# Banded attention inside a feed-forward kernel: probabilities turned and split block by block, one padded product for the sinks, normalisation on GpSimd

## The chip, the cores and the metric

The kernel runs on one core of one Trainium2 chip. The metric is the device time of one execution in microseconds (us). Engines are named as in the profile: PE is TensorE, DVE VectorE, ACT ScalarE, POOL GpSimd, SP SyncE, which here only issues DMAs.

## What is computed

The inputs of the attention are q, k and v of shape (4, 8, 768, 64); every query sees the first `n_sink` keys (4 here; the kernel holds up to 16) and the last `window` keys up to itself (128). The 8 heads of a token, side by side, are a row of 512 numbers, and go through two feed-forward layers, with 2048 hidden numbers each.

```python
scores = scale * np.matmul(q, k.transpose(0, 1, 3, 2))
keep = is_sink | in_window            # pos < n_sink, or 0 <= rel < window
scores = np.where(keep, scores, -1000000000.0)
scores = scores - np.max(scores, axis=-1, keepdims=True)
a = np.exp(scores)
a = a / (np.sum(a, axis=-1, keepdims=True) + 1e-09)
attn_out = np.matmul(a, v)
x = attn_out.transpose(0, 2, 1, 3).reshape(B * S, H * D)
h = x @ w_in                          # first layer
x = (h - np.tanh(h)) @ w_out
h = np.maximum(x @ w_in2, 0.0)        # second layer
out = (h * h) @ w_out2
```

## The kernel before, in words

**Two parts of a number.** Most products are made with float32r operands: a float32 is split into a high part (a copy to float32r, on ACT) and a low part (the difference, on DVE or POOL), and a product is the sum of three: high by high, high by low, low by high. Heads 0 to 15 (`n < FULL`) use plain float32 in the attention; the 48 later heads use the parts.

**Tiles.** The 3072 tokens are cut into 8 tiles of T = 384 tokens, half a batch each. An even tile holds the first half of a sequence (`half` = 0), an odd tile the second. For each tile the first layer runs over 16 hidden chunks of 128: `mm1` gives a chunk (12 products of 384 columns into a bank of PSUM, two halves of 6), `act` takes tanh on ACT (`t`), `h - tanh` on DVE, and splits it (`gs`: ACT copy, DVE or POOL difference), `mm2` adds the chunk into four banks `acc` (12 products, two halves of 6), one chunk behind. Then all tiles go through the second layer in the same way, with no attention any more.

**The stream of heads.** PE executes its instructions in program order, and the order is written out: before each half of `mm1` and each half of `mm2` a hook calls `tick(pos)`, which puts the attention's steps of that place there. A chunk has four places, a head eight, so that the 8 heads of the next tile fill the 16 chunks of a tile. Heads of even tiles (half 0) pass in the odd tiles 1, 3, 5, heads of odd tiles (half 1) in tile 0 (plain float32) and in tiles 2, 4, 6. The stream runs OFF = 10 places ahead of the tile that needs it. On the other engines a scheduler sets the order.

**One head.** Its 384 queries are three units u of 128. A unit of kind 2 (all three of half 1, only the last of half 0) sees two blocks of 128 keys, the one before and its own, and 16 sink keys: 272 columns. Kind 0 sees one block, kind 1 two blocks of which the first is where the sinks lie. `split_qk` and `split_v` split q, k and v of the next head (ACT copies, POOL differences). `score` makes two products into `ps_s`, adds the mask on DVE; `exp` exponentiates on ACT with the row sums in `sm`. `recip` and `norm` normalise on DVE. For a unit of kind 2 `norm` **folds**: since a query sees of the block before only keys above its own place, and of its own block only keys up to it, both blocks' probabilities are added into 128 columns (L290, L291). `trans` transposes the folded block on PE into `ps_t`, splits it in two copies (ACT L349, DVE L350), and POOL unfolds it with the mask `above` (L353, L354). The sinks' probabilities of all units lie side by side in `s.sink` and are transposed at once, 32 rows for each unit. `av` makes for each unit one product of 256 columns (high and low P side by side) for each block of V (lhs: high V in the upper, low V in the lower half of its columns), and one product with 16 rows for the sinks (`pts`, `v_k`) ahead of them. `gather` adds the parts up into `xf` for units 0 and 1 together, and for unit 2 (ACT L408, DVE L409, L412); every second head `xf` is split into `x`, the next tile's input.

Of the kernel before, what the change touches and what calls it, by code (L numbers as in the profile page):

```python
# [47 lines left out]
def scalars(c):  # L48
    """n_sink and window as float32 on every partition."""
# [11 lines left out]
def band_fits(c):  # L61
    """1 if n_sink and window fit the banded path, else 0."""
# [10 lines left out]
def keep_masks(c, pool, shape_n, base, tag):  # L73
    """Where query base+p sees key j, 1.0, else 0.0."""
# [16 lines left out]
def band_masks(c):  # L91
    """What is added to the scores of the first, the second and any later query block."""
# [26 lines left out]
    c.above = cp.tile([P, 1, P], F32, tag="above", name="above")  # L119
    nc.vector.tensor_scalar(c.above[:, 0, :], d, 0.0, None, ALU.is_gt)  # L120
# [22 lines left out]
def split(c, dst, src, lo_eng):  # L143
    """float32 as the sum of two float32r parts."""
# [5 lines left out]
class Weights:  # L150
    """The chunks of one layer's two matrices, on chip as float32r parts."""
# [18 lines left out]
class Heads:  # L170
    """Banded attention of one head and one tile after another, cut into steps."""
# [14 lines left out]
    def load(self, n):  # L186
# [11 lines left out]
        if n % (2 * H) == 0 and n > 0:  # L198
            self.vs_raw = c.sb.tile([P, DM], I32, tag="w_bit", name="w_bit", bufs=3).bitcast(F32)[: 3 * SR].rearrange(
                "p (h d) -> p h d", d=D)  # L200
            nc.sync.dma_start(self.vs_raw, c.vs[b])

    def split_qk(self, n):
        c, nc, s = self.c, self.c.nc, self.st[n]
        j, b, half, h = self.coords(n)
        nk = (3 + half) * KB - NS
# [10 lines left out]
    def split_v(self, n):  # L217
        c, nc, s = self.c, self.c.nc, self.st[n]
        j, b, half, h = self.coords(n)
        if n < FULL:  # L220
            return
        nb = 3 + half
# [18 lines left out]
    def bank(self, n, i, tag, spare):  # L241
        """A bank; the banks of the products serve too while there are none."""
# [4 lines left out]
    def score(self, n, u):  # L247
        c, nc, s = self.c, self.c.nc, self.st[n]
        half = self.coords(n)[2]
        if u == 0:  # L250
            if n < H:
                t, pt = (slot(c, "wo", FC - 1 - (2 * n + i) % TMP, F32).rearrange("p a c -> p (a c)") for i in range(2))
                s.p = t[:, : 3 * WN].rearrange("p (u w) -> p u w", w=WN)
                s.pt0 = pt.rearrange("p (b q) -> p b q", q=P)
# [504 lines left out]
```

## Time and profile before

| | |
|---|---|
| median of 3 runs | 1366.1 us (1365.66 to 1366.31) |
| span of the profiled execution | 1364.8 us |
| PE busy | 1302.1 us, 95% of the span |
| DVE, ACT, POOL busy | 855.0, 629.3, 443.9 us (63%, 46%, 33%) |
| tile 0, us from the span's start | 44 to 167.9 |
| tile 1 (heads of half 0 in it) | 167.9 to 258.0 |
| tile 2 (heads of half 1 in it) | 258.0 to 360.3 |
| tiles 3, 5 and tiles 4, 6 | 90.1 us and 102.3 us each |
| last tile of layer one, and layer two | from 745.2 us |

The span is what the profiler saw from the first instruction to the last; the timed runs are 1.3 us longer. A tile's stretch is read by the first `mm1` product of each tile. In the view of windows, busy times of the engines are in the order PE, PE's weight loads, DVE, ACT, POOL, and the number behind them is the granted clock of TensorE as a share of full speed.

### The profile page before, as it was taken

What the parts mean: (1) busy time and instruction counts of PE and PEld (TensorE: products, weight loads), DVE (VectorE), ACT (ScalarE), POOL (GpSimd) and SP (SyncE); (2) the same over time, 40 slices, a digit from 0 to 9 for tenths busy, and PEclk for the clock granted to TensorE, in tenths of its full rate; (3) what the DMA queues carried; (4) which work ended last, traced back from release to release, by engine and by line L of the source; (5) the groups of instructions that cost most, each with busy time, mean ns of one, the idle gap of its engine ahead of it and who ended that gap; (6) DMA issues with size and microseconds to landing.
All of it is one profiled execution on the core that took longest, in us unless ns stands there. A gap on an engine that the chain in (4) does not pass through costs nothing.

```text
span 1364.8 us, 19807 instructions
## 1 busy us (share of the span) xinstructions
PE 1302.1 (95%) x7080; PEld 1185.5 (87%) x7080; DVE 855.0 (63%) x2012; ACT 629.3 (46%) x1604; POOL 443.9 (33%) x463
## 2 busy tenths in 40 slices
PE   7999999989999989999989989999999999999998
PEld 6788899878899888998889987799999999999997
DVE  8999688888788887878785799722222222222222
ACT  6666556545555545665544455423232223232222
POOL 1555534556434556435553254301010101010000
PEclk9999999999999999999999999999999999999999
DMA  9631211211211211212102851010100000000000
GB/s 365 247 115 58 91 52 56 79 38 46 70 49 56 79 34 46 70 53 75 60 1 84 273 182 61 12 35 12 36 18 29 23 25 24 24 13 24 10 15 26
DMA packets 31836, 90.87 MB, mean 67 GB/s; under 512 B 3792, under 2 KB 11984, under 8 KB 31728
## 3 DMA queue, kind: packets, MB, share of 16 engines
q1 hardware_dynamic: 31728, 89.51, 19.6%
q8 instruction: 58, 0.95, 0.3%
q14 instruction: 50, 0.41, 0.1%
HBM read 76.91 MB, written 12.58 MB: 66 GB/s over the span
## 4 chain that ended last, share of the span: by engine, by line
PE 59%; DVE 28%; ACT 6%; issue 5%; DMA 1%; SPq 0%; DVEq 0%; ACTq 0%
PE acc L504 18%; PE ps_h L470 13%; PE acc L502 6%; PE ps_v L470 5%; PE ps_t L470 5%; PE ps_s L470 5%; PE ps_v L382 4%; DVE p L291 4%; DVE p L290 4%; DVE w_bit L137 3%; DVE gs L147 3%; DVE sm L283 3%; DVE w_bit L136 2%; ACT p L278 2%; DVE w_bit L135 2%
## 5 line engine op out<-in xcount | busy, mean ns | idle before, releaser
L470 PE MATMUL ps_h<-x,wi 128*128 128x384 f32 x1776 | 363.1, 343 | 1.0 <-DVE t L482 1.0
L470 PEld LDWEIGHTS ps_h<-x,wi 128*128 128x128 f32 x1776 | 302.5, 188 | 6.5 <-DVE t L482 1.7
L502 PE MATMUL acc<-gs,wo 128*128 128x384 f32 x1440 | 288.4, 341 | 1.1 <-DVE gs L147 1.1
L502 PEld LDWEIGHTS acc<-gs,wo 128*128 128x128 f32 x1440 | 244.0, 188 | 2.5 <-DVE gs L147 1.4
L147 POOL TENSOR_TENSOR x<-xf,x 128x384 fp32r<-128x384 f32 x36 | 38.2, 1070 | 366.4 <-ACT x L146 366.2
L504 PE MATMUL acc<-wo,gs 128*128 128x512 f32 x576 | 146.3, 397 | 4.2 <-DVE gs L147 3.6
L147 DVE TENSOR_TENSOR gs<-t,gs 128x384 fp32r<-128x384 f32 x168 | 114.0, 679 | 56.8 <-ACT gs L146 56.8
L504 PE MATMUL acc<-wo,p 128*128 128x512 f32 x576 | 143.4, 393 | 1.2 <-DVE p L147 0.9
L278 ACT ACTIVATE p<-p,nm 128x272 f32<-128x272 f32 (+1 forms) x168 | 84.5, 503 | 104.2 <-DVE nm L271 97.2
L504 PEld LDWEIGHTS acc<-wo,gs 128*128 128x128 f32 x576 | 107.9, 190 | 26.0 <-DVE gs L147 4.6
L504 PEld LDWEIGHTS acc<-wo,p 128*128 128x128 f32 x576 | 107.1, 188 | 21.0 <-DVE p L147 1.4
L146 ACT ACTIVATE gs<-t 128x384 fp32r<-128x384 f32 x184 | 95.5, 519 | 43.6 <-DVE t L485 38.1
L353 POOL TENSOR_TENSOR pt<-pt,above 128x256 fp32r<-128x256 f32 x96 | 70.7, 737 | 133.9 <-DVE pt L350 133.9
L481 ACT ACTIVATE t<-ps_h 128x384 f32<-128x384 f32 x116 | 56.8, 490 | 73.0 <-PE ps_h L470 73.0
L470 PE MATMUL ps_t<-x,wi 128*128 128x384 f32 x432 | 81.7, 337 | 0.0
L470 PE MATMUL ps_v<-x,wi 128*128 128x384 f32 x432 | 81.6, 337 | 0.0
L470 PE MATMUL ps_s<-x,wi 128*128 128x384 f32 x432 | 81.5, 336 | 0.0
L470 PEld LDWEIGHTS ps_t<-x,wi 128*128 128x128 f32 x432 | 77.0, 189 | 2.7
L354 POOL TENSOR_TENSOR pt<-pt 128x256 fp32r<-128x256 f32 x96 | 76.8, 800 | 7.5
L470 PEld LDWEIGHTS ps_v<-x,wi 128*128 128x128 f32 x432 | 76.7, 188 | 2.8
L470 PEld LDWEIGHTS ps_s<-x,wi 128*128 128x128 f32 x432 | 76.6, 188 | 2.8
L271 DVE CUSTOM_DVE_ANT_0 p<-ps_s,m 128x128 f32<-128x128 f32 (+1 forms) x144 | 59.1, 410 | 27.7 <-PE ps_s L270 26.1
(140 smaller groups left out, 2083.8 us busy)
## 6 DMA issues: line engine op xcount, KB each, us to landing
qkv<-in_a_dram SPq DMA_DIRECT2D x32, 608.0 KB, 4.0
wi<-in_w_in_dram SPq DMA_DIRECT2D x32, 512.0 KB, 5.7
wo<-in_w_out_dram SPq DMA_DIRECT2D x32, 512.0 KB, 5.8
qkv<-in_a_dram SPq DMA_DIRECT2D x24, 504.0 KB, 3.6
x<-o SPq DMA_DIRECT2D x32, 192.0 KB, 1.9
xf<-x SPq DMA_DIRECT2D x32, 192.0 KB, 2.4
out_dram<-o SPq DMA_DIRECT2D x24, 256.0 KB, 2.1
wi<-in_a_dram SPq DMA_DIRECT2D x8, 504.0 KB, 8.2
```

The source lines that it names most:

```text
L146: nc.scalar.activation(dst[:, 0, :], src, AF.Copy)
L147: lo_eng.tensor_tensor(dst[:, 1, :], src, dst[:, 0, :].bitcast(F32), ALU.subtract)
L271: nc.vector.tensor_tensor_reduce(out=s.p[:, u, :w], in0=sc[:, :w], in1=self.masks[kind], op0=ALU.add, op1=ALU.min, scale=-SCALE, scalar=3. ...
L278: self.mark[n] = nc.scalar.activation(s.p[:, u, :w], s.p[:, u, :w], AF.Exp, bias=s.nm[:, u : u + 1], scale=-1.0, accum_out=s.sm[:, u : u + 1])
L290: nc.vector.tensor_scalar(s.p[:, u, KB:], s.p[:, u, KB:], s.sm[:, u : u + 1], None, ALU.mult)
L291: nc.vector.scalar_tensor_tensor(s.p[:, u, KB:], s.p[:, u, :P], s.sm[:, u : u + 1], s.p[:, u, KB:], ALU.mult, ALU.add)
L353: nc.gpsimd.tensor_tensor(a, b.bitcast(F32), c.above.to_broadcast([P, 2, P]), ALU.mult)
L354: nc.gpsimd.tensor_tensor(b, b.bitcast(F32), a.bitcast(F32), ALU.subtract)
L470: nc.tensor.matmul(h[:, :T], w[:, a, kc, :], x[kc][:, b, :], start=(kc == 0 and i == 0), stop=(kc == KC - 1 and i == 2))
L481: c.last_a = nc.scalar.activation(t, h[:, :T], AF.Tanh)
L502: nc.tensor.matmul(acc[m][:, :T], w[:, a, ts(m, P)], gs[:, b, :], **st)
L504: nc.tensor.matmul(acc[m], gs[:, b, ts(m, P)], w[:, a, :], **st)
```

## The change

P is no longer folded. A head of half 0 has five blocks of probabilities of 128 by 128, one of half 1 six (`parts`), ordered by block of keys. They are transposed three at a time at places 0 and 2 of the next head (`trans`), each group into one bank, and evicted by one ACT copy of 384 columns (high) and one DVE difference (low), into one buffer `pt` with high P and low P apart. At place 4 the sinks' columns of each unit are transposed 64 rows high (`trans_sinks`); the high part goes to rows 0 to 63 of `pts`, the low part to rows 64 to 127, where the sink rows of V stand a second time, the rest being zeros (`layout`). `av` at places 3 and 5 makes for each block of V two products, one with high P and one with low P, over the queries of both units that see it (256 columns, or 128 columns at the ends, where the low one has only 66 of V's columns as outputs), all into one bank for the head. `av_sinks` at place 6 is a single product with 128 rows. `gather` is one ACT copy and one DVE addition of 384 columns. `norm` adds 1e-9 on ACT, takes the reciprocal on DVE, and multiplies on POOL, three instructions a head, all issued at place 5. The low part of `x` moves from DVE to POOL. OFF becomes 11; `pt` and `pts` have one buffer in place of two, and `o`, the buffer of the products' last eviction, two in place of three. The first weight conversions wait for head 3 in place of head 2.

```diff
-SR = 32               # rows, of which the sinks take the first, of a query block's sink probabilities when transposed
+SR = 64
...
-TRANS = ((1, 3, 5), (0, 3, 6))
-AV = ((4, 6, 9), (3, 7, 9))
-OFF = 10              # places by which the stream of heads runs ahead of the tile that needs it
+OFF = 11
...
-    def recip(self, n):
-        nc.vector.tensor_scalar(s.sm, s.sm, 1.0e-9, None, ALU.add)
+    def norm(self, n):
+        c, nc, s = self.c, self.c.nc, self.st[n]
+        nc.scalar.activation(s.sm, s.sm, AF.Identity, bias=c.eps)
         self.markd[n] = nc.vector.reciprocal(s.sm, s.sm)
...
+        for u in range(3):
+            w = self.width(n, u)
+            nc.gpsimd.tensor_scalar(s.p[:, u, :w], s.p[:, u, :w], s.sm[:, u : u + 1], None, ALU.mult)
+
+    def parts(self, n):
+
+        half = self.coords(n)[2]
+        out = []
+        for kb in range(3 + half):
+            for u in (kb - half, kb - half + 1):
+                if 0 <= u < 3:
+                    out.append((u, 0 if self.kind(n, u) == 0 or u + half != kb else KB, kb))
+        return out
+
+    def evict(self, n, hi, lo, src):
+
+        nc = self.c.nc
+        nc.scalar.activation(hi, src, AF.Copy)
+        if n >= FULL:
+            nc.vector.tensor_tensor(lo, src, hi.bitcast(F32), ALU.subtract)
+
+    def trans(self, n, g):
+
+        c, nc, s = self.c, self.c.nc, self.st[n]
+        bl = self.parts(n)
+        if g == 0 and n >= H:
+            pt = c.sb.tile([P, 2, 6, P], F32R, tag="pt", name="pt", bufs=1)
+            s.pt = pt if n >= FULL else pt.bitcast(F32)
+        lo, hi = 3 * g, min(3 * g + 3, len(bl))
+        tp = self.bank(n, g, "ps_t", "acc").rearrange("p (a q) -> p a q", q=P)
+        for i in range(lo, hi):
+            u, col, _ = bl[i]
+            nc.tensor.transpose(tp[:, i - lo, :], s.p[:, u, col : col + P], c.ident)
+        self.evict(n, s.pt[:, 0, lo:hi, :], s.pt[:, 1, lo:hi, :] if n >= FULL else None, tp[:, : hi - lo, :])
...
+        for i, u in enumerate(us):
+            nc.tensor.transpose(tp[:rows, i, :], s.p[:, u, P : P + rows], c.ident)
...
+            s.ps = c.sb.tile([P, 3, P], F32R, tag="pts", name="pts", bufs=1)[:, : len(us), :]
...
+        self.evict(n, s.ps[:rows], s.ps[SR:], tp[:rows, : len(us), :])
...
+            st = dict(start=(kb == 0), stop=False, skip_group_check=True)
...
+            v = s.vt[:, kb].rearrange("p a d -> p (a d)")
+            nc.tensor.matmul(s.av[:, cols], v, s.pt[:, 0, blocks, :], **st)
+            st["start"] = False
+            m = P if len(idx) > 1 else D + 2
+            nc.tensor.matmul(s.av[:m, cols], v[:, :m], s.pt[:, 1, blocks, :], **st)
...
+        nc.tensor.matmul(out, lhs, s.ps, start=False, stop=True, skip_group_check=True)
...
+        t = c.sb.tile([D, T], F32, tag="t_av", name="t_av", bufs=2)
+        nc.scalar.activation(t, s.av[D:, :T], AF.Copy)
+        nc.vector.tensor_tensor(dst, s.av[:D, :T], t, ALU.add)
...
+            split(c, x, self.xf, c.nc.gpsimd)
...
+            if k == 5:
+                self.norm(n)
+        m = n - 1
+        if 0 <= m < last:
+            if k in (0, 2):
+                self.trans(m, k // 2)
+            if k == 4:
+                self.trans_sinks(m)
+            if k in (3, 5):
+                self.av(m, k // 5)
...
+                self.av_sinks(m)
+                self.gather(m)
+                self.finish(m)
...
-                o = c.fp.tile([P, 512], F32, tag="o", name="o", bufs=3)
+                o = c.fp.tile([P, 512], F32, tag="o", name="o", bufs=2)
...
-                with tc.issue_after(heads.mark[2].ins), tc.issue_after(heads.markd[2].ins):
+                with tc.issue_after(heads.mark[3].ins), tc.issue_after(heads.markd[3].ins):
...
+    vs = np.zeros((B, P, H, D), v.dtype)
+    vs[:, :NS] = vs[:, SR : SR + NS] = v[:, :, :NS].transpose(0, 2, 1, 3)
+    arrays["vs"] = vs
```

The order of instructions on PE, before, for most of a head of half 1 in tile 2 (L470 is `mm1`, L502 `mm2`, L269 and L270 the scores, L327 and L330 transposes, L382 the products with V; the sizes are inputs' rows by columns):

```order
L470 MATMUL ps_h<-x,wi_776 128x384 x6
L382 MATMUL ps_v<-pts,v_k 128x256
L382 MATMUL ps_v<-pt,v_s 128x256 x2
L470 MATMUL ps_h<-x,wi_776 128x384 x6
L269 MATMUL ps_s<-k_h,q_s 128x272
L270 MATMUL ps_s<-k_l,q_s 128x272
L327 MATMUL ps_t<-ident,p 128x128
L330 MATMUL ps_t<-ident,p 96x128
L502 MATMUL acc<-gs,wo_734 128x384 x6
L382 MATMUL ps_v<-pts,v_k 128x256
L382 MATMUL ps_v<-pt,v_s 128x256 x2
L502 MATMUL acc<-gs,wo_734 128x384 x6
```

And of the change, from the second group of transposes of such a head to its product with the sinks (L437 is `mm1`, L469 `mm2`, L260 and L261 the scores, L308 and L321 transposes, L349, L352 and L363 the products with high P, low P and the sinks):

```order
L308 MATMUL ps_t<-ident,p 128x128 x3
L469 MATMUL acc<-gs,wo_1324 128x384 x6
L349 MATMUL ps_v<-pt,v_s 128x128
L352 MATMUL ps_v<-pt,v_s 66x128
L349 MATMUL ps_v<-pt,v_s 128x256
L352 MATMUL ps_v<-pt,v_s 128x256
L437 MATMUL ps_h<-x,wi_1440 128x384 x6
L260 MATMUL ps_s<-k_h,q_s 128x272
L261 MATMUL ps_s<-k_l,q_s 128x272
L321 MATMUL ps_t<-ident,p 64x128 x3
```

The three blocks of one product with the sinks and two with V, each into a bank that waits for the gathering of the last, became two groups of four products with V and one product with the sinks; transposes went from four to nine.

On ACT before, around the splitting of q, k for the next head in tile 2 (L481 is tanh, L212 and L214 the high parts of q and k, L278 exp, L146 the high part of `gs`, L349 of P, L408 the copy in `gather`):

```order
L481 ACTIVATE t<-ps_h 128x384
L212 ACTIVATE q_s<-qkv 128x384
L278 ACTIVATE p,sm<-p,nm 128x272
L146 ACTIVATE gs<-t 128x384
L214 ACTIVATE k_h<-qkv 128x560
L349 ACTIVATE pt<-ps_t 128x128
L408 ACTIVATE t_av<-ps_v 64x256
```

And of the change, at the same stretch of a head (L269 is exp, L206 the high part of q, L448 tanh, L274 the addition of 1e-9 to the sums, L217 the high part of v, L141 that of `gs`, L376 the copy in `gather`, L293 a group's high part of P):

```order
L269 ACTIVATE p,sm<-p,nm 128x272
L206 ACTIVATE q_s<-qkv 128x384
L448 ACTIVATE t<-ps_h 128x384
L274 ACTIVATE sm<-sm,eps 128x3
L217 ACTIVATE v_s<-qkv 128x4x64
L141 ACTIVATE gs<-t 128x384
L376 ACTIVATE t_av<-ps_v 64x384
L293 ACTIVATE pt<-ps_t 128x384
```

The addition to the sums, on which the reciprocal and the multiplications wait, stands behind a tanh, and the copy of v ahead of `gs`.

On POOL before, for most of a head in tile 2 (L353 and L354 unfold P, L213, L215 and L225 are the low parts of q, k and v):

```order
L354 TENSOR_TENSOR pt<-pt 128x256
L213 TENSOR_TENSOR q_s<-qkv,q_s 64x384
L215 TENSOR_TENSOR k_l<-qkv,k_h 128x560
L353 TENSOR_TENSOR pt<-pt,above 128x256
L354 TENSOR_TENSOR pt<-pt 128x256
L353 TENSOR_TENSOR pt<-pt,above 128x256
L354 TENSOR_TENSOR pt<-pt 128x256
L225 TENSOR_TENSOR v_s<-qkv,v_s 128x4x64
```

And of the change (L209, L207 and L218 are the low parts of k, q and v, L278 `norm`, L142 the low part of `x`):

```order
L209 TENSOR_TENSOR k_l<-qkv,k_h 128x560
L207 TENSOR_TENSOR q_s<-qkv,q_s 64x384
L218 TENSOR_TENSOR v_s<-qkv,v_s 128x4x64
L278 TENSOR_SCALAR p<-p,sm 128x272 x3
L142 TENSOR_TENSOR x<-xf,x 128x384
L209 TENSOR_TENSOR k_l<-qkv,k_h 128x560
```

The six unfolding instructions of a head are gone, and three multiplications stand behind the low part of v.

## Rows read from the trace of the kernel before

**Rows 1.** The page: span, and DMAs of the results with us to landing.

```profile
span 1364.8 us, 19807 instructions
...
out_dram<-o SPq DMA_DIRECT2D x24, 256.0 KB, 2.1
```

**Rows 2.** Windows (columns as told above): start, tile 0, tile 1, tile 2.

```profile
0.00:44.00 44.00, 35.99 (x204) 27.42 (x205) 36.27 (x146) 29.97 (x95) 9.87 (x15) 1.00 0.88 341
44.00:167.90 123.90, 115.61 (x663) 103.60 (x663) 106.58 (x211) 75.86 (x179) 68.43 (x53) 1.00 0.32 115
167.90:258.00 90.10, 87.08 (x522) 82.78 (x521) 73.64 (x208) 53.49 (x159) 38.32 (x44) 1.00 0.19 61
258.00:360.30 102.30, 94.77 (x537) 84.97 (x537) 83.65 (x221) 54.56 (x161) 59.61 (x70) 1.00 0.16 51
```

**Rows 3.** Waits of PE in tile 2: us in total, times, longest.

```profile
PE ps_v L382 <- DVE xf L412: 7.5, 8, 1.2
```

**Rows 4.** Waits of PE in tile 1.

```profile
PE ps_v L382 <- DVE xf L412: 3.0, 8, 1.4
```

**Rows 5.** Timeline of PE in tile 1: start, us, work.

```profile
232.46 0.28 PE L269 MATMUL ps_s<-k_h,q_s 128*128 128x272 f32 x1
...
232.71 2.25 PE L502 MATMUL acc<-gs,wo 128*128 128x384 f32 x12
234.79 0.27 PE L327 MATMUL ps_t<-ident,p 128*128 128x128 f32 x1
```

**Rows 6.** Timeline of PE and ACT at the end of tile 1.

```profile
254.23 0.51 PE L470 MATMUL ps_h<-x,wi 128*128 128x384 f32 x2
...
254.73 0.35 PE L382 MATMUL ps_v<-pts,v_k 16*128 16x256 f32 x1
...
255.35 0.27 PE L327 MATMUL ps_t<-ident,p 128*128 128x128 f32 x1
...
255.38 1.31 PE L470 MATMUL ps_h<-x,wi 128*128 128x384 f32 x6
...
256.73 0.49 ACT L481 ACTIVATE t<-ps_h 128x384 f32<-128x384 f32 x1 [0.71 <-PE ps_h L470]
...
257.12 0.52 ACT L212 ACTIVATE q_s<-qkv 128x384 fp32r<-128x384 f32 x1
```

**Rows 7.** The chain that ended last, in tile 0: start, us, what.

```profile
49.39 0.33 PE ps_t L327 x3
...
89.30 2.02 DVE w_bit L136 x2
...
96.17 0.60 DVE w_bit L136
...
133.99 2.03 DVE w_bit L136 x2
```

**Rows 8.** Groups of instructions on POOL: busy us, mean ns of one, idle before.

```profile
L147 POOL TENSOR_TENSOR x<-xf,x 128x384 fp32r<-128x384 f32 x36 | 38.2, 1070 | 366.4 <-ACT x L146 366.2
...
L354 POOL TENSOR_TENSOR pt<-pt 128x256 fp32r<-128x256 f32 x96 | 76.8, 800 | 7.5
...
L225 POOL TENSOR_TENSOR v_s<-qkv,v_s 128x256 fp32r<-128x256 f32 x24 | 17.4, 724 | 6.2 <-ACT v_s L224 6.2
L225 POOL TENSOR_TENSOR v_s<-qkv,v_s 128x192 fp32r<-128x192 f32 x24 | 14.8, 617 | 35.2 <-ACT v_s L224 35.2
...
masks.py:199 POOL TENSOR_SCALAR_AFFINE_SELECT ident<-ident 128x128 f32<-128x128 f32 x1 | 0.3, 292 | 0.0
```

**Rows 9.** Timeline of POOL in tile 0.

```profile
104.08 1.42 POOL L147 TENSOR_TENSOR gs<-t,gs 128x384 fp32r<-128x384 f32 x1 [1.98 <-issue]
```

**Rows 10.** Timeline at the end of the kernel: evictions of the last products.

```profile
1356.84 0.60 ACT L513 ACTIVATE o<-acc 128x512 f32<-128x512 f32 x1 [3.08 <-PE acc L504]
...
1358.20 0.60 ACT L513 ACTIVATE o<-acc 128x512 f32<-128x512 f32 x1 [0.76 <-PE acc L504]
```

More of the change, by code (lines that the diff above doesn't have):

```diff
@@ L204, in split_qk @@
         c, nc, s = self.c, self.c.nc, self.st[n]
-        j, b, half, h = self.coords(n)
-        nk = (3 + half) * KB - NS
+        nk = (3 + self.coords(n)[2]) * KB - NS
         if n < FULL:
@@ L296, in norm_sinks @@
-    def norm_sinks(self, n):
-        c, nc, s = self.c, self.c.nc, self.st[n]
-        if n < FULL:
-            return
-        us = [u for u in range(3) if self.folded(n, u)]
-        off = 0 if us[0] == 0 else P
-        s.nk = SR * len(us)
-        s.sink = s.p[:, 0, off : off + s.nk]
-        nc.vector.tensor_tensor(s.sink.rearrange("p (u k) -> p u k", k=SR), s.p[:, us[0] :, P : P + SR],
-                                s.sm[:, us[0] :, None].to_broadcast([P, len(us), SR]), ALU.mult)
-    def folded(self, n, u):
-        return n >= FULL and self.kind(n, u) == 2
@@ L385, in gather @@
-    def gather(self, n, u):
-        c, nc, s = self.c, self.c.nc, self.st[n]
-        j, b, half, h = self.coords(n)
-        if h % 2 == 0 and u == 1:
-            self.xf = c.sb.tile([P, T], F32, tag="xf", name="xf", bufs=2)
-        if n < FULL:
-            if u == 2:
-                nc.scalar.activation(self.xf[D * (h % 2) : D * (h % 2) + D, :], s.av[:D, :T], AF.Copy)
-        else:
-            self.add_up(n, u)
-        if u == 2:
-            if h % 2 == 1:
-                x = c.xp.tile([P, 2, T], F32R, tag="x", name="x", bufs=8)
-                split(c, x, self.xf, nc.vector if n >= H else nc.gpsimd)
-                self.x.setdefault(j, [None] * KC)[h // 2] = x
-            del self.st[n]
@@ new lines, in with_sinks, with trans_sinks @@
+    def with_sinks(self, n):
+        return [u for u in range(3) if self.kind(n, u) == 2]
+    def trans_sinks(self, n):
+        c, nc, s = self.c, self.c.nc, self.st[n]
+        us = self.with_sinks(n)
+        full = n < FULL
+        rows = P if full else SR
+        tp = self.bank(n, 0, "ps_t", "acc").rearrange("p (a q) -> p a q", q=P)
+        for i, u in enumerate(us):
+            nc.tensor.transpose(tp[:rows, i, :], s.p[:, u, P : P + rows], c.ident)
+        if n < H:
+            s.ps = s.pt[:, 0, 5:6, :]
+        else:
+            s.ps = c.sb.tile([P, 3, P], F32R, tag="pts", name="pts", bufs=1)[:, : len(us), :]
+            if full:
+                s.ps = s.ps.bitcast(F32)
+        self.evict(n, s.ps[:rows], s.ps[SR:], tp[:rows, : len(us), :])
@@ new lines, in av @@
+    def av(self, n, g):
+        c, nc, s = self.c, self.c.nc, self.st[n]
+        bl = self.parts(n)
+        if g == 0:
+            s.av = self.bank(n, n, "ps_v", "acc")
+        for kb in range(bl[-1][2] + 1):
+            idx = [i for i, x in enumerate(bl) if x[2] == kb]
+            if (idx[-1] >= 3) != g:
+                continue
+            u0 = bl[idx[0]][0]
+            cols = slice(u0 * P, (u0 + len(idx)) * P)
+            blocks = slice(idx[0], idx[-1] + 1)
+            st = dict(start=(kb == 0), stop=False, skip_group_check=True)
+            if n < FULL:
+                nc.tensor.matmul(s.av[:, cols], s.v[:, kb : kb + 2, :].rearrange("p a d -> p (a d)"),
+                                 s.pt[:, 0, blocks, :], **st)
+                continue
+            v = s.vt[:, kb].rearrange("p a d -> p (a d)")
[3 more added lines that the diff above has]
+            nc.tensor.matmul(s.av[:m, cols], v[:, :m], s.pt[:, 1, blocks, :], **st)
@@ L412, in add_up, with gather @@
-        nc.vector.tensor_tensor(dst, s.av[:D, :m, 0, :], t[:, :m, :], ALU.add)
+        us = self.with_sinks(n)
+        out = s.av[:, us[0] * P : 3 * P]
+        if n < FULL:
+            lhs = self.vsink[:, h : h + 2, :].rearrange("p a d -> p (a d)")
+        else:
+            lhs = self.vsink[:, h].rearrange("p a d -> p (a d)")
+        nc.tensor.matmul(out, lhs, s.ps, start=False, stop=True, skip_group_check=True)
+    def gather(self, n):
+        c, nc, s = self.c, self.c.nc, self.st[n]
+        h = self.coords(n)[3]
+        if h % 2 == 0:
+            self.xf = c.sb.tile([P, T], F32, tag="xf", name="xf", bufs=2)
+        dst = self.xf[D * (h % 2) : D * (h % 2) + D, :]
+        if n < FULL:
+            nc.scalar.activation(dst, s.av[:D, :T], AF.Copy)
+            return
+        t = c.sb.tile([D, T], F32, tag="t_av", name="t_av", bufs=2)
+        nc.scalar.activation(t, s.av[D:, :T], AF.Copy)
+        nc.vector.tensor_tensor(dst, s.av[:D, :T], t, ALU.add)
@@ L414, in tick, with finish @@
+    def finish(self, n):
+        c = self.c
+        j, b, half, h = self.coords(n)
+        if h % 2 == 1:
+            x = c.xp.tile([P, 2, T], F32R, tag="x", name="x", bufs=8)
+            split(c, x, self.xf, c.nc.gpsimd)
+            self.x.setdefault(j, [None] * KC)[h // 2] = x
+        del self.st[n]
     def tick(self, pos):
```

151 lines of the change are left out of this document (23 added, 128 removed).

## The prediction

> **What bounds the kernel now.** I read the windows of the first stages first [rows 2]. PE is busy for 94.77 of the 102.30 us of tile 2 and for 87.08 of the 90.10 us of tile 1, at a granted clock of 1.00, which is the 2.4 GHz level, throughout. So after tile 0 a tile lasts as long as PE's own work and its few waits, and DVE (83.65 and 73.64 us) is the nearest other engine. Tile 0 lasts 123.90 us, with DVE at 106.58: another bound, to which I come below. From 745 us on there is no attention, and the change touches nothing there but the buffers of the last eviction.
>
> Second, PE's waits. In tile 2 they come to 7.5 us in 8 waits, all at the first product of a block into `ps_v` that the addition into `xf` has not yet released [rows 3]; in tile 1 to 3.0 us [rows 4]. That is .94 us a head of half 1 and .38 a head of half 0.
>
> Third, what one PE instruction costs, from start to start in the timeline. Twelve products of 384 columns take from 232.71 to 234.79, .174 each [rows 5], so a tile's 384 products of `mm1` and `mm2` alone are 66.9 us. Two score products of 256 to 272 columns take from 232.46 to 232.71, .12 each [rows 5]. Three transposes take .33, .11 each [rows 7]. The block of one product with the sinks (16 rows) and two with V is dearer than three times .12: two `mm1` products start at 254.23, so that they end their issue at 254.58, and the next transpose starts at 255.35; the block took .77 without any wait in it [rows 6], .41 more than .36.
>
> **The change, per head of half 1** (24 heads, tiles 2, 4, 6; 12.79 us a head now, from 102.30/8). Off: three such blocks, -2.32; the waits on `xf`, -.94, since one bank now gathers a whole head and the next head's first product comes five places later. On: four products of 256 columns, +.48; the product with the sinks, 384 columns, +.17; four products of 128 columns, which I take at .12 (the transposes, 128 columns too, took .11; half the price of 256 columns, .06, is the other bound), +.48; five more transposes, +.55. This is -1.58, if nothing new waits. I assume here that the .41 belongs to the product with 16 rows, of which none is left.
>
> A new wait is likely, since the normalisation leaves DVE for the end of a queue. Call E the end of the first half chunk's products at place 5; it is 256.69 in [rows 6]. There tanh began .04 behind E and the next ACT instruction at E+.43. In the changed order that next one is the addition of 1e-9 (.1), then the copy of v (about .40 for 256 columns, by .52 for 384): done at about E+.96. POOL then splits v, .72 [rows 8], to E+1.73, and only then normalises, three units one after another.
>
> What one multiplication by a column on POOL costs, no row shows. POOL's differences of two inputs took .617 for 192 and .724 for 256 columns [rows 8]: .0017 a column and a fixed .30, which gives .75 for 272, or .78 with the .80 of L354. The only operation with one input, 128 wide, took .29 [rows 8], which is the fixed part alone. So .30 to .78; I take .50, between the two. The unit 0 is then ready at E+2.28. Its successor is pushed: DVE's difference for `gs` falls there, and when both engines read two inputs from SBUF they slow each other: a POOL difference of 384 columns took 1.42 beside a DVE weight conversion against a mean of 1.07 [rows 8, 9], and the conversion's pairs took 1.01 each against .60 alone [rows 7]. With that .35, unit 1 is ready at E+3.16, PE hears of it at 3.25.
>
> PE on its side issues after E the sinks' product, .17, twelve products, 2.09, the next scores, .24, and two transposes, .22; since its last product ends its issue .16 before E, it comes to the third transpose, the first of unit 1, at E+2.56. It waits .69 a head. Behind it in PE's queue stands all of the next chunk, so nothing fills this; DVE's eviction of the low part comes later by the same.
>
> Sum: -1.58 +.69 = -.89; with rounding -.90 a head, **-21.6 us** in 24 heads.
>
> **Per head of half 0** (24 heads; 11.26 us a head now, from 90.10/8). Off: one block with sinks, -.78, three other products, -.36, the wait, -.38. On: four products of 256 columns, +.48; two of 128 and the sinks' 128, +.36; one transpose, +.11. The wait at the norm: the first unit is 128 wide (.30), v's difference .617 [rows 8], and unit 1 is wanted at the second transpose, so it is due at E+2.40 and comes at about E+2.84: +.44. Sum -.14, **-3.4 us**.
>
> **Tile 0** (heads 8 to 15 in plain float32). The chain returns to the weight conversions of DVE, whose pairs come at 89.30 and 133.99 three heads apart, 14.90 us a head, and they are long just where POOL works [rows 7, 9]. The change takes the multiplications and part of the evictions off DVE and puts three POOL instructions and nothing else in their place, so DVE's own time falls and that in which POOL slows it rises, by .5 each. I take 14.2 to 15.0 a head in place of 14.9, **-2** (-5 to +6). Start: the heads of tile 0 have no products beside them, PE is busy 35.99 of 44.00 and DVE 36.27, and the DMA queues .88 [rows 2], so less DVE work meets the loads: **0**, -5 to +5, as the first product of layer one now stands one place later in the stream.
>
> **The end.** With two buffers `o` the third eviction of the last tile, at 1358.20, waits for the first, which starts at 1356.84 and takes .60 [rows 10], and for its DMA, 2.1 to land [rows 1]: 1359.5, **+1.4**. In the other tiles of layer two the next tile's work goes on meanwhile. Edits at nothing: `gather`'s one copy of 384 columns, the low part of `x` on POOL (1.07 every second head), behind the norms; POOL loses six instructions a head, three of them of .80 [rows 8], so it has the room (59.61 of 102.30 busy [rows 2]). That cover is gone if the norms cost far more (below).
>
> **The sum** is -21.6 -3.4 -2 +1.4 = -25.6: a span of 1339.2 in place of 1364.8 [rows 1], and 1.3 more by the timed runs: 1340.5, say **1341 us**. The 128-column products at .06 would take 10 more off (24 by .24 and by .18).
>
> On the unknown price: the Trainium skill, "GPSIMD Engine Reference", section "4.1 Engine selection", puts elementwise work on VectorE and calls GpSimd about twice slower for two inputs and about line-rate for one. By the first the change is a bad trade, by the second the multiplication would be near the lower bound above. No row here shows an instruction of this kind, so the sum keeps its bounds.
>
> **The rivals.** *All hidden.* ACT may bring the copy of v earlier, or a multiplication may take .30: then both new waits go, -.69 and -.44 a head, 27 us more: 1314. For it: POOL is then less busy than now; against: `gs` and v stand ahead. Chance .14.
>
> *Norms late (slower).* If a multiplication costs as much as a difference of two inputs, .78, unit 1 comes .56 later and tile 0's POOL work grows as well. Each .1 costs two times .1 for 24 heads of half 1, .15 for 24 of half 0 (its first unit is narrow), and .26 a head in tile 0: 4.8+3.6+2.1 = 10.5 us. From .50 to .78 that is 29 us: about 1370. It decides from .74 on. For it: all POOL work of 256 columns that is seen takes .72 or more. Chance .18.
>
> *The short product is not the cause.* If the .41 of a block comes not from 16 rows but from any change of shape between products, it comes back with the products of 66 columns (two a head of half 1, one of half 0): +.82 and +.41, 29.5 us: about 1370. Against it: transposes and scores between products of other widths go at .11 and .12. For it: only this block is seen with it. Chance .12. The Trainium skill, "TensorE: Matmul & The Clock Gate", section "Why this matters for your kernels", says that a product with 32 rows takes the time of one with 128, which would leave the 16 rows without blame; the block's .77 against .36 rather speaks against it.
>
> **How the numbers follow.** The forecast itself .50, all hidden .14, norms late .18, the shape .12, other causes (a race for `ps_t`, one buffer of `pt`, tile 0 by more than bound) .06. A difference under 0.2% (2.7 us) could not be told from none. Faster: .50 + .14, and .05 of the two rivals near 1370 and of the rest; same: .08; slower: .23, the most of the two rivals. The range goes from the all-hidden case, 1314, to 1374, a few us past the two slow ones; the forecast's own range is 1325 to 1356.
>
> **What would show it.** Right: tile 2 at about 95 us and tile 1 at about 89; no wait on `xf` at `ps_v`; waits of PE at the second or third transpose on POOL's multiplication, .4 to .7 a head; multiplications at .4 to .6; the sinks' product at .17 to the next. Wrong: multiplications over .74; products of 66 columns with gaps; tile 0 over 130 us; waits on DVE's low parts of P at `av`, because `pt` has one buffer and DVE writes it after ACT.

## The result: slower by 0.65%

The changed kernel takes 1375.86 us (median of 4 runs, 1372.14 to 1376.34) against 1366.2 before: a ratio of 1.0065, 95% interval 1.0051 to 1.0079. The forecast was 1341 with a range up to 1374. The profiled execution of the changed kernel took 1376.34, with a span of 1374.5, 9.7 more than before [rows 1].

The busy times on its page answer to the table of before: PE and DVE have less to do, POOL 63.8 us more, and the span is longer all the same.

```profile
PE 1294.6 (94%) x7152; PEld 1196.3 (87%) x7152; DVE 633.9 (46%) x1376; ACT 643.9 (47%) x1588; POOL 507.7 (37%) x491
```

Where the time went is read best by stages that begin exactly with the first `mm1` product of a tile. Behind the start, the windows of [rows 2] and the table of before do not: they were cut some 4 us later (167.90 for 163.84 and so on; 745.2 for 738.70 at the last), so that tile 0 has 123.90 us there and 119.72 here, and the other tiles differ by a few tenths. The kernel before, cut exactly (its start is 44.12 us): tile 0, tile 1, tile 2, tile 7.

```profile
44.12:163.84 119.72, 111.43 (x638) 99.42 (x637) 103.96 (x203) 73.34 (x172) 67.64 (x52) 1.00 0.32 115
163.84:253.53 89.69, 86.67 (x522) 82.78 (x521) 72.90 (x205) 52.99 (x158) 36.01 (x42) 1.00 0.18 60
253.53:356.14 102.61, 95.08 (x538) 85.19 (x537) 83.95 (x222) 54.35 (x159) 60.71 (x72) 1.00 0.17 53
...
738.70:805.47 66.77, 65.36 (x374) 64.43 (x373) 49.28 (x73) 32.99 (x65) 21.30 (x17) 1.00 0.78 248
```

The changed kernel, its start and the same four tiles:

```profile
0.00:61.76 61.76, 41.59 (x180) 29.03 (x181) 24.51 (x104) 35.88 (x113) 33.19 (x42) 0.93 0.66 251
61.76:188.15 126.39, 107.55 (x571) 93.63 (x570) 88.78 (x158) 78.91 (x189) 95.86 (x80) 0.98 0.31 110
188.15:277.81 89.66, 86.98 (x541) 84.39 (x540) 43.33 (x122) 52.49 (x150) 49.26 (x53) 1.00 0.20 62
277.81:373.20 95.39, 91.82 (x575) 88.38 (x574) 48.22 (x122) 57.11 (x151) 54.24 (x53) 1.00 0.18 56
...
741.35:814.26 72.91, 67.86 (x373) 66.90 (x373) 49.38 (x72) 32.15 (x64) 20.25 (x16) 0.95 0.72 224
```

Start +17.6, tile 0 +6.7, tile 1 nothing, tile 2 -7.2, tile 7 +6.1. With tiles 4 and 6, which lose 7.2 each too, and .9 us behind tile 7, this is the whole difference. The gain in the heads of half 1 is there. Three other stages take it back: the start and tile 0, which serve the first 16 heads, and tile 7, which has no attention beside it.

PE's waits in the changed kernel, the start (two rows), tile 0 (two), tile 2, tile 7 (us in total, times, longest).

```profile
PE ps_t L308 <- POOL wo L278: 6.9, 12, 1.3
...
PE acc L308 <- POOL wo L278: 4.4, 8, 0.9
...
PE ps_v L363 <- ACT pts L293: 6.5, 5, 2.1
...
PE ps_t L308 <- POOL p L278: 4.6, 3, 3.6
...
PE ps_t L308 <- POOL p L278: 3.2, 7, 0.5
...
PE acc L469 <- ACT o L480: 3.7, 1, 3.7
```

In the start and in tiles 0 and 2 the name is the same: the multiplication of L278 on POOL. Its price, in groups by shape (busy us, mean ns, idle before), for heads 8 to 63 (`p`) and for the first eight (`wo`):

```profile
L278 POOL TENSOR_SCALAR p<-p,sm 128x272 f32<-128x272 f32 x144 | 146.9, 1032 | 8.2 <-DVE sm L275 8.2
...
L278 POOL TENSOR_SCALAR wo<-wo,sm 128x272 f32<-128x272 f32 x16 | 16.0, 1012 | 0.0
...
L278 POOL TENSOR_SCALAR wo<-wo,sm 128x128 f32<-128x128 f32 x8 | 5.5, 691 | 19.0 <-DVE sm L275 15.1 <-PE acc L363 2.1 <-PE ps_v L363 1.8
```

1.03 us for 272 columns: twice my .50, and beyond the .78 that I took for the upper bound.

### The profile page after: what moved, and what is told of

Its sections match the earlier page's. It is cut to its first block, busy times and chain, and to the rows that moved or that the text cites. A ratio compares the mean times of both kernels' runs of the same rounds, so it can differ in the third digit from the quotient of the medians.

```text
span 1374.5 us, 19167 instructions
## 1 busy us (share of the span) xinstructions
PE 1294.6 (94%) x7152; PEld 1196.3 (87%) x7152; DVE 633.9 (46%) x1376; ACT 643.9 (47%) x1588; POOL 507.7 (37%) x491
## 5 line engine op out<-in xcount | busy, mean ns | idle before, releaser
L437 PE MATMUL ps_h<-x,wi 128*128 128x384 f32 x1776 | 365.6, 344 | 0.0
L437 PEld LDWEIGHTS ps_h<-x,wi 128*128 128x128 f32 x1776 | 307.4, 190 | 4.5 <-DVE t L449 1.3
L469 PE MATMUL acc<-gs,wo 128*128 128x384 f32 x1440 | 301.4, 346 | 9.4 <-ACT o L480 6.0
L469 PEld LDWEIGHTS acc<-gs,wo 128*128 128x128 f32 x1440 | 247.6, 189 | 15.9 <-ACT o L480 7.7
L142 POOL TENSOR_TENSOR x<-xf,x 128x384 fp32r<-128x384 f32 x64 | 66.9, 1051 | 345.1 <-ACT x L141 342.9
L278 POOL TENSOR_SCALAR p<-p,sm 128x272 f32<-128x272 f32 (+1 forms) x168 | 167.2, 1008 | 8.4 <-DVE sm L275 8.4
L209 POOL TENSOR_TENSOR k_l<-qkv,k_h 128x416 fp32r<-128x416 f32 (+1 forms) x48 | 59.5, 1239 | 228.9 <-ACT k_h L208 228.8
L142 DVE TENSOR_TENSOR gs<-t,gs 128x384 fp32r<-128x384 f32 x168 | 105.1, 626 | 62.8 <-ACT gs L141 62.8
L141 ACT ACTIVATE gs<-t 128x384 fp32r<-128x384 f32 x184 | 96.4, 524 | 78.1 <-DVE t L452 38.2
L262 DVE CUSTOM_DVE_ANT_0 p<-ps_s,m 128x272 f32<-128x272 f32 (+1 forms) x168 | 70.3, 418 | 126.6 <-PE ps_s L261 116.4
L449 DVE TENSOR_TENSOR t<-ps_h,t 128x384 f32<-128x384 f32 x116 | 64.7, 558 | 87.1 <-ACT t L448 87.1
L293 ACT ACTIVATE pt<-ps_t 128x384 fp32r<-128x384 f32 (+1 forms) x112 | 51.9, 463 | 85.6 <-PE ps_t L308 85.6
L308 PE MATMUL ps_t<-ident,p 128*128 128x128 f32 x312 | 65.1, 288 | 23.3 <-POOL p L278 22.6
L269 ACT ACTIVATE p<-p,nm 128x272 f32<-128x272 f32 (+1 forms) x168 | 83.3, 496 | 3.2 <-DVE nm L262 3.2
L437 PE MATMUL ps_v<-x,wi 128*128 128x384 f32 x432 | 83.1, 341 | 0.0
L437 PE MATMUL ps_s<-x,wi 128*128 128x384 f32 x432 | 82.2, 338 | 0.0
L437 PE MATMUL ps_t<-x,wi 128*128 128x384 f32 x432 | 81.5, 336 | 0.0
L437 PEld LDWEIGHTS ps_v<-x,wi 128*128 128x128 f32 x432 | 78.4, 192 | 2.8
```

The source lines that it names most:

```text
L141: nc.scalar.activation(dst[:, 0, :], src, AF.Copy)
L142: lo_eng.tensor_tensor(dst[:, 1, :], src, dst[:, 0, :].bitcast(F32), ALU.subtract)
L209: nc.gpsimd.tensor_tensor(s.kl[:, :nk], s.k[:, :nk], s.kh[:, :nk].bitcast(F32), ALU.subtract)
L262: nc.vector.tensor_tensor_reduce(out=s.p[:, u, :w], in0=sc[:, :w], in1=self.masks[kind], op0=ALU.add, op1=ALU.min, scale=-SCALE / 2 if ful ...
L269: self.mark[n] = nc.scalar.activation(s.p[:, u, :w], s.p[:, u, :w], AF.Exp, bias=s.nm[:, u : u + 1], scale=-1.0, accum_out=s.sm[:, u : u + 1])
L278: nc.gpsimd.tensor_scalar(s.p[:, u, :w], s.p[:, u, :w], s.sm[:, u : u + 1], None, ALU.mult)
```

## The experiments

**Multiplications of the first heads on DVE.**

```diff
+            eng = nc.vector if n < FULL else nc.gpsimd
-            nc.gpsimd.tensor_scalar(s.p[:, u, :w], s.p[:, u, :w], s.sm[:, u : u + 1], None, ALU.mult)
+            eng.tensor_scalar(s.p[:, u, :w], s.p[:, u, :w], s.sm[:, u : u + 1], None, ALU.mult)
```

> The changed kernel with the multiplications of heads 0 to 15 back on DVE, everything else as changed. Theory A (the first products of layer one begin at 61.76 instead of 44.12 us, and tile 0 lasts 126.4 instead of 119.7, because three multiplications of .7 to 1.0 us on GpSimd stand between exp and the transposes of a head): first product at 44 to 49, tile 0 at 112 to 121, total 1348 to 1358. Theory B (it is the new order, three blocks transposed together after the sums of all units, whatever engine multiplies): first product stays at 56 to 62, total 1368 to 1374. Theory C (half of it is the clock, 0.79 to 0.85 in two stretches of the start): first product at 52 to 56 with the clock still low.

Measured 1349.51 (ratio to before .9870, .9853 to .9886), inside theory A's range. Start and tile 0:

```profile
0.00:46.34 46.34, 36.88 (x181) 28.30 (x181) 33.04 (x133) 36.19 (x116) 10.91 (x16) 0.98 0.90 346
46.34:163.60 117.26, 104.75 (x571) 94.27 (x570) 82.47 (x177) 76.52 (x185) 87.14 (x58) 0.98 0.32 115
```

The start gives back 15.4 of its 17.6 us, tile 0 goes below the kernel before. Only the engine of an operation changed, so theory B falls; with the start at 46.34 and its clock at .98, C does too. On DVE the same operation takes about a third of the time:

```profile
L279 DVE TENSOR_SCALAR p<-p,sm 128x272 f32<-128x272 f32 x24 | 7.4, 357 | 0.2
```

**The same part alone, in the kernel before.**

```diff
-        nc.vector.tensor_scalar(s.p[:, u, :w], s.p[:, u, :w], s.sm[:, u : u + 1], None, ALU.mult)
+        eng = nc.gpsimd if n < FULL else nc.vector
+        eng.tensor_scalar(s.p[:, u, :w], s.p[:, u, :w], s.sm[:, u : u + 1], None, ALU.mult)
```

> The kernel before with one part of the change alone: the multiplications of heads 0 to 15 on GpSimd. Theory A: the first product of layer one moves from 44 to 52 to 62, tile 0 grows by 3 to 8, total 1377 to 1392. Theory B: no more than 3 us later at the start, total 1364 to 1370.

Measured 1386.5 (1.0141, 1.0120 to 1.0161), a total inside theory A's range:

```profile
0.00:61.64 61.64, 44.99 (x206) 32.43 (x206) 33.97 (x126) 32.72 (x97) 37.32 (x43) 0.89 0.63 243
61.64:182.42 120.78, 111.99 (x638) 101.22 (x637) 88.57 (x174) 71.81 (x170) 87.97 (x73) 0.99 0.32 114
```

The start grows by 17.5, as in the changed kernel and without its order of blocks. Tile 0 grows by 1.1 only, under the 3 to 8 expected. In the changed kernel the same move of the engine costs 9.1 there (126.39 against 117.26). Both kernels have the slow multiplication in tile 0; only the changed one also has its three units in one queue ahead of transposes three at a time, but which of its differences makes the other 8 us was not tried.

**Two buffers of the evictions, in the kernel before.**

```diff
-                o = c.fp.tile([P, 512], F32, tag="o", name="o", bufs=3)
+                o = c.fp.tile([P, 512], F32, tag="o", name="o", bufs=2)
```

> The kernel before with two buffers of the last evictions in place of three, nothing else. Theory A (the third eviction of the sixth-to-seventh tile waits for the DMA of the first, which is slow beside the weights' loads, PE stands still and then runs at half the clock for some 6 us): last tile of layer one from 66.8 to 72 to 74 us, the others within .6, the end +.5 to +1.5, total 1371 to 1375. Rival (the loss in that tile comes from the later attention stream, not from the buffers): 66.8 stays, total 1366 to 1368.

Measured 1376.08 (1.0067, 1.0051 to 1.0084): 9 us more, so the edit that I had put at 1.4 costs as much alone as the whole change. But not where theory A had it. A wait of ACT's evictions for a store, which the kernel before has not (whole run: us, times, longest), and tile 7:

```profile
ACT o L513 <- DMA x<-o: 6.7, 8, 2.7
...
746.81:814.19 67.38, 65.58 (x374) 64.35 (x374) 49.78 (x73) 32.90 (x65) 21.28 (x17) 1.00 0.77 245
```

Tile 7 grows by .6, tiles 1 to 6 by .9 to 2.4 each (tile 2 the most, 105.05). I read this as evictions that wait for a store and hold up the attention's steps behind them on ACT and DVE; only the wait itself is shown. So two buffers do not explain the changed kernel's tile 7 by themselves, and the rival, that buffers cost nothing, is wrong too.

**A third buffer in the changed kernel,** for the third eviction of a tile in layer one.

```diff
+                if l == 0 and m == 2:
+                    o = c.fp.tile([P, T], F32, tag="o3", name="o3", bufs=1)
+                else:
+                    o = c.fp.tile([P, 512], F32, tag="o", name="o", bufs=2)
...
-        t = c.sb.tile([D, T], F32, tag="t_av", name="t_av", bufs=2)
+        t = c.sb.tile([D, T], F32, tag="t_av", name="t_av", bufs=1)
```

> The changed kernel with a third buffer for the evictions of layer one (paid for by one buffer of the copy in the gathering in place of two). Theory A as for the kernel before with two: last tile of layer one back to 66.8 to 67.5, no low clock there, total 1368 to 1371. Rival: 72 to 73 stays, total 1374 to 1377.

Measured 1373.97 (1.0056, 1.0039 to 1.0072), tile 7 at 71.75: the rival was nearer. PE's wait had only gone to the fourth eviction, 3.4 us on DVE's copy in place of 3.7 on ACT's. The timeline at tile 6's eviction, early in tile 7, shows a store that lands late. In the kernel before, the issues of the stores and the fourth eviction:

```profile
745.25 1.54 SPq L515 DMA_DIRECT2D x<-o  x3
...
748.12 0.56 DVE L511 COPY o<-acc 128x384 f32<-128x384 f32 x1 [1.76 <-DMA x<-o]
```

And in the changed kernel, with a load of layer two's weights right ahead of the stores, and the third eviction, which waits:

```profile
747.98 0.33 SPq L155 DMA_DIRECT2D wi<-in_w_in_dram  x1
...
748.37 1.25 SPq L482 DMA_DIRECT2D x<-o  x2
...
753.98 0.49 ACT L480 ACTIVATE o<-acc 128x384 f32<-128x384 f32 x1 [5.25 <-DMA x<-o]
```

Before, the eviction that waits for the first store begins 2.9 us after that store's issue at 745.25; now 5.6 us after 748.37, with two weight loads issued at 744.83 and 747.98. When PE went on at 754.52, after 3.7 us of waiting, it did so at half the clock: the granted clock is .50, the 1.2 GHz level, until 760.

```profile
754.00:756.00 2.00, 1.48 (x5) 1.48 (x6) 1.02 (x2) 1.29 (x3) 0.00 (x0) 0.50 0.42 157
```

**A place for each eviction of tiles 6 and 7,** on top of the first experiment.

```diff
+                if l == 0 and j >= NT - 2:
+                    if m == 0:
+                        ob = c.sb.tile([P, 2, 6, P], F32R, tag="pt", name="pt", bufs=1).bitcast(F32)
+                        ob = ob.rearrange("p a b q -> p (a b q)")
+                    o = ob[:, m * T : (m + 1) * T]
+                else:
+                    o = c.fp.tile([P, 512], F32, tag="o", name="o", bufs=2)
```

> The kernel with plain heads on DVE, and four places of their own for the evictions of tiles 6 and 7, in the memory of the probabilities, which no head needs any more there. A third buffer for the fourth eviction's predecessor had left the last tile of layer one at 71.75. Theory A (the order of DMAs on the issuing queue changed, weights of layer two are now loaded beside the first evictions' stores, which land late; with a place for each no eviction waits for a landing): tile 7 from 72.2 to 66.7 to 68, no stretch at half the clock there, total 1343 to 1346. Rival (the products of that tile wait for the loads themselves, or PE is slowed by something else): over 70, total 1348 to 1350.

Measured 1344.01 (.9826, .9809 to .9844), 5.5 under the first experiment:

```profile
716.67:783.16 66.49, 65.08 (x373) 64.45 (x373) 49.26 (x72) 32.11 (x63) 20.27 (x16) 1.00 0.80 245
```

Theory A holds: tile 7 is at the kernel before's length, with the clock at 1.00. The loss needs both, few buffers and stores that land late; without the first the second is harmless. The order of DMAs on the issuing queue was not varied by an experiment, but the traces vary it, and it is not layer two's weights alone. In tile 1 of the fastest kernel (below), one store goes out at 168.44 and three at 172.17, right behind a load of q, k and v at 171.79. The two kinds of store (number, KB each, us to landing):

```profile
x<-o SPq DMA_DIRECT2D x1, 192.0 KB, 1.8
...
x<-o SPq DMA_DIRECT2D x3, 192.0 KB, 4.0
```

The load itself took 3.9. Over the whole run the median of the stores is 1.9 us in the kernel before and 3.4 in the changed one, where in each of tiles 1 to 6 the first two stores go out right behind such a load:

```profile
x<-o SPq DMA_DIRECT2D x32, 192.0 KB, 1.9
...
x<-o SPq DMA_DIRECT2D x32, 192.0 KB, 3.4
```

So stores land late in all these tiles; in tiles 1 and 2 PE pays .3 and .4 us for it, in tile 7 it pays 3.7 and then the clock. Which of the change's edits put the loads there was not tried.

**The low part of v behind the multiplications on POOL,** on top of the first experiment.

```diff
-            eng.tensor_scalar(s.p[:, u, :w], s.p[:, u, :w], s.sm[:, u : u + 1], None, ALU.mult)
+            self.markn = eng.tensor_scalar(s.p[:, u, :w], s.p[:, u, :w], s.sm[:, u : u + 1], None, ALU.mult)
...
-                self.split_v(n + 1)
+                with self.c.tc.issue_after(self.markn.ins):
+                    self.split_v(n + 1)
```

> The kernel with plain heads on DVE, and on GpSimd the low part of v behind the three multiplications of a head instead of ahead of them; nothing else moves. Theory A (PE's wait at the third transpose is the end of a queue on GpSimd: v's .73 us, then two multiplications of 1.05): the wait shrinks by up to .7 a head, tiles 2, 4 from 95.4 to 89.7 to 91, tiles 1, 3, 5 from 89.8 to 85.5 to 87, total 1318 to 1330 against 1349.5. Rival (the wait is only the name of a later one: exp, tanh and the copy of v on ACT set the time): under 1 us a tile, total 1345 to 1350.

Measured 1327.59 (.9709, .9687 to .9730). Tile 2:

```profile
253.06:341.65 88.59, 88.59 (x575) 88.52 (x574) 46.78 (x122) 57.23 (x151) 51.87 (x53) 1.00 0.19 61
```

Tile 2 gives back 6.8 us (95.41 in the first experiment), .85 a head, more than the .7 expected: PE is busy from end to end and has no wait on POOL left. The theory holds there. Tiles 1, 3 and 5 missed their range (90.05, 88.74, 88.84). In tile 1 PE now waits 2.8 us for DVE's eviction of the last tile's products, which itself waits 3.1 us for a store, and the clock falls to a mean of .98.

**All multiplications on DVE.** (The diff is `nc.gpsimd` to `nc.vector` in `norm`.)

> The changed kernel with the multiplications of all heads on DVE. Theory A (the wait of PE at the transposes costs .5 to .8 a head and is all due to the multiplications on GpSimd): tiles 2, 4 at 88.5 to 91, tiles 1, 3, 5 at 85 to 87.5, total 1318 to 1330. Rival (DVE, busy 48 of 95 us, gets the wait instead, since its differences for gs and for P queue behind three more instructions of .4): tiles 2, 4 at 93 to 97, total 1343 to 1352.

Measured 1322.31 (.9671, .9653 to .9688). Tile 1 takes 85.34, and tile 2:

```profile
248.08:338.46 90.38, 88.90 (x575) 88.50 (x574) 56.45 (x147) 56.64 (x153) 29.66 (x29) 1.00 0.19 59
```

Theory A holds: 4.4 us less a tile of half 0, 5.0 a tile of half 1. DVE has the room, 56 of 90 us.

**Sixteen rows in the product with the sinks.** The low part of the sinks' probabilities is left out of the sum.

```diff
+        rows = P if n < FULL else NS
-        nc.tensor.matmul(out, lhs, s.ps, start=False, stop=True, skip_group_check=True)
+        nc.tensor.matmul(out, lhs[:rows], s.ps[:rows], start=False, stop=True, skip_group_check=True)
```

> The changed kernel with 16 rows in the product with the sinks in place of 128 for the 48 later heads; the low part of the sinks' probabilities is left out of the sum. Theory A (the .41 of a block of the kernel before is the price of a product with 16 rows among such with 128): the stretch between the products ahead of and behind it grows from .17 by .25 to .45, tiles by 2 to 3.6 us, total 1388 to 1396. Rival (as 128 rows; the block's price came from elsewhere): under .05 a head, total 1373 to 1377.

Measured 1376.62 in one run: the rival's total, but the theory's mechanism. In the changed kernel's timeline, the six products ahead of the sinks' product, the six behind it, and the next:

```profile
305.61 1.26 PE L469 MATMUL acc<-gs,wo 128*128 128x384 f32 x6
...
306.88 1.20 PE L469 MATMUL acc<-gs,wo 128*128 128x384 f32 x6
...
307.92 1.20 PE L437 MATMUL ps_h<-x,wi 128*128 128x384 f32 x6
```

And with 16 rows:

```profile
305.76 1.26 PE L470 MATMUL acc<-gs,wo 128*128 128x384 f32 x6
...
307.33 1.32 PE L470 MATMUL acc<-gs,wo 128*128 128x384 f32 x6
308.49 0.68 PE L438 MATMUL ps_h<-x,wi 128*128 128x384 f32 x3
```

From the six ahead to the six behind it is 1.57 in place of 1.27, .30 more; the six behind then take 1.16 in place of 1.04, so that the whole stretch is 2.73 in place of 2.31, .42 more. That is the .41 of the prediction's block. Tile 2 grows by .3 alone (95.67): I read this as PE coming later to the transposes, where it waits for POOL anyway. A cost ahead of a wait is paid out of the wait.

**The parts together.** All multiplications on DVE, the third buffer, and the places for tiles 6 and 7:

> All multiplications on DVE, four places for the evictions of tiles 6 and 7, and a third buffer for those of tiles 0 to 5. If the waits on the last evictions (9.7 us at PE in the kernel with all multiplications on DVE, some with low clock behind) are due to buffers alone: tile 7 at 66.5 to 68, tiles 2 and 4 at 87.5 to 89.5, total 1312 to 1317 against 1322.3. Rival (with the store of an eviction landing late, a third buffer gives nothing in tiles 0 to 5): only tile 7 shortens, total 1316 to 1319.

Measured 1314.42 (.9612, .9596 to .9628). Tile 7 is 66.42; tiles 2 and 4 hardly change (90.13 and 89.75), so that part of the expectation was wrong. It is the buffers still: three do not suffice for four evictions there. In tile 2 the fourth, on DVE, waits for a store, and PE 1.3 us for it (in tile 4 2.4 and .9):

```profile
DVE o L486 <- DMA x<-o: 2.7, 1, 2.7
```

The same places and buffer with v behind the multiplications on POOL:

> As the kernel with the low part of v behind the multiplications on GpSimd, with the same places and third buffer. By buffers alone: tile 7 at 66.5 to 68, tiles 1, 3, 5 from 88.8 to 85.5 to 86.5 and tiles 2, 4 at 88 to 89, total 1308 to 1316 against 1327.6. Rival (tiles 1, 3, 5 stay at 88 to 89 since DVE evicts the fourth block late, whatever buffer it has): total 1319 to 1323.

Measured 1312.63 (.9598, .9582 to .9614), the fastest. Tiles 2 and 7 take 88.80 and 66.46, tile 1:

```profile
164.18:249.69 85.51, 85.03 (x541) 84.51 (x540) 42.73 (x122) 52.64 (x150) 48.26 (x53) 1.00 0.20 64
```

In tiles 1, 3 and 5 the third buffer is worth 3.2 to 4.5 us, which the waits on POOL had hidden: in tile 1 of the changed kernel it gave .4.

## Why the prediction was wrong, point by point

Against the forecast span of 1339.2 the profiled one is 35.3 longer: 17.6 in the start, 8.7 in tile 0, 6.1 in tile 7, 3.3 in the tiles of half 0, none in those of half 1, and .5 less at the end.

**"Start: 0", +17.6.** This is the step that failed most. I read that PE and DVE were both busy for 36 of 44 us and concluded that less DVE work can only help. The heads of tile 0 have no products beside them, so a new length in one head's chain is paid. Three multiplications on POOL, .69 and two of 1.01 by their groups, stand there between the reciprocal and the transposes, and had to be added to the chain as I did for the later heads. PE waits 11.3 us for them in the start (6.9 and 4.4), where it waited .4 for DVE's before. On DVE the three took 1.07 in the first experiment, so an estimate by these groups is 1.64 a head, 13.1 in eight heads. The one part alone gives +17.5 in the kernel before. The clock takes part: the granted clock is .85 and .79 in two stretches of the changed start, which is at most (1-.85)10 + (1-.79)11.76 = 4 us; PE had waited on POOL just before.

```profile
30.00:40.00 10.00, 7.17 (x30) 5.04 (x29) 4.63 (x15) 5.86 (x19) 5.13 (x5) 0.85 1.02 403
50.00:61.76 11.76, 9.71 (x43) 7.52 (x43) 5.37 (x15) 8.22 (x24) 9.04 (x9) 0.79 0.16 45
```

**"Tile 0: -2", +6.7.** Without the multiplications on POOL it is -2.5, which was the forecast's direction for the relief of DVE. With them it is 9.1 more. The term had the price, .50 against 1.03, and the chain, which I had counted as DVE's alone, wrong. But the price does not make the 9.1 by itself, since the same multiplications cost 1.1 in this tile in the kernel before; the rest stays open.

**"The end: +1.4", and the other tiles at nothing.** At the end the third eviction does wait as forecast: it starts 2.74 us behind the first (1368.63 and 1365.89) in place of 1.36. From the first to the end of the span it is 8.61 in place of 7.96, so the end cost .7. I looked for two buffers only there. Tile 6's evictions, whose stores go out right behind a load of layer two's weights, cost 6.1 in tile 7.

**Half 1: -21.6, measured -21.6** (tiles 2, 4, 6 together), but by terms that were off in both directions: that the sum is right is luck. Tile 2 at 95.39 and tile 1 at 89.66 came as I had written for the case that the forecast is right, together with multiplications over .74, which I had written for the case that it is wrong. The work itself came to -1.75 a head where nothing waits (tile 4 with v behind the multiplications, 88.59 against 102.56), for -1.58 forecast: products of 128 columns took .06, the lower of my two bounds, and not .12, and three transposes went in .25 (300.77 to 301.02), .08 each and not .11.

```profile
302.15 0.22 PE L349 MATMUL ps_v<-pt,v_s 128*128 128x128 f32 x1
302.21 0.22 PE L352 MATMUL ps_v<-pt,v_s 128*66 128x128 f32 x1
302.27 0.33 PE L349 MATMUL ps_v<-pt,v_s 128*128 128x256 f32 x1
```

The wait came to .85 a head for .69, by the experiment that moves v. (The view of waits has only 3.2 us in tile 2, since it counts from the modelled end of PE's product before.) Its working was wrong twice, and the two nearly cancelled:

```profile
306.22 1.02 POOL L207 TENSOR_TENSOR q_s<-qkv,q_s 64x384 fp32r<-64x384 f32 x1
...
307.31 0.73 POOL L218 TENSOR_TENSOR v_s<-qkv,v_s 128x256 fp32r<-128x256 f32 x1
...
308.02 3.14 POOL L278 TENSOR_SCALAR p<-p,sm 128x272 f32<-128x272 f32 x3
...
309.34 0.44 PE L308 MATMUL ps_t<-ident,p 128*128 128x128 f32 x2
...
310.28 0.33 PE L308 MATMUL ps_t<-ident,p 128*128 128x128 f32 x1 [0.50 <-POOL p L278]
```

E, the end of the chunk's `mm1` products, is 305.42 here (six from 304.11, 1.31 us). POOL had q's low part to do first, so v began at E+1.89 (I had E+1.01), and two multiplications took 2.1 in place of 1.0. But PE issues 18 products between E and the transposes, not the 12 I counted: place 5 lies ahead of `mm2`, not of the second half of `mm1`, when the stream runs 11 places ahead. So PE was late too. The mechanism, the end of POOL's queue, was right: the experiment that moves v shows it.

**Half 0: -3.4, measured -.1.** The wait here came to .55 a head for .44 (4.4 us a tile, by the kernel with all multiplications on DVE), and the work without waits to -.52 for -.58 (85.51 in tile 1 of the fastest kernel).

**The rivals.** *Norms late* was the right one of the slow ones, with its price too low (1.03, not .78; from the .80 for 256 columns it should have been .83, still too low) and its heaviest place, the start, missing. Its rule of 10.5 us for each .1 overstated the tiles, where PE came later as well, and left out the start. The rule of the Trainium skill, "GPSIMD Engine Reference", section "4.1 Engine selection", that such work belongs on VectorE was the better guide here; its rough line-rate for one input does not agree with 1.03 us beside DVE's .36, and the measurement decides. *The short product is not the cause* is refuted: the product of 66 columns goes at .06, and 16 rows do cost .42 more. *All hidden* put the time at 1314: the kernel without most of the new waits takes 1312.63. That the two are so near is in part luck, since with its 128-column products at .06 that rival would have stood 10 us lower.

## What to carry to other kernels

Add a moved operation to the chain of every stage that executes it, the stage without cover first: one rule for the steady tiles does not price the start. When an operation's price on an engine is in no trace, the bounds from other operations of that engine can both be too low; try the operation first, or keep the sum open upward. And when buffers become fewer, look at each place where their release is a store, above all one that goes out right behind a load, and not only at the kernel's last instruction: where PE needs the result soon, the wait is paid there, and again through the clock.

## What the runs showed of the hardware that was not expected

On POOL a multiplication by a column, with one tensor from SBUF, is dearer than a difference of two tensors of about the same size: 1.03 us for 272 columns (.96 where DVE is idle) against .72 to .80 for 256 [rows 8]; on DVE it takes .36. It slows DVE less than a difference on POOL does. DVE's difference for `gs` takes .56 with POOL idle. In the changed kernel one that fell on the low part of v (307.31 to 308.04) and the start of the multiplications took .95; in the kernel with v behind them, one that fell inside the multiplications (280.06 to 282.91) took .72, and all 47 such took .61 in the mean:

```profile
307.51 0.95 DVE L142 TENSOR_TENSOR gs<-t,gs 128x384 fp32r<-128x384 f32 x1 [0.51 <-ACT gs L141]
...
280.23 0.72 DVE L142 TENSOR_TENSOR gs<-t,gs 128x384 fp32r<-128x384 f32 x1 [0.51 <-ACT gs L141]
```

Among products with all 128 rows, one with 16 rows costs .42 us more, of which .12 falls on the six products behind it. The Trainium skill, "TensorE: Matmul & The Clock Gate", section "Why this matters for your kernels", has a 32-row product at the time of a 128-row one; no run here has 32 rows, and at 16 the measurement differs.
